# Linear attention and a gated feed-forward on one TensorE: the first two weight loads in parts of a tile of their own

## The chip, the cores and the metric

The kernel runs on one core of a Trainium2 chip. The metric is the device time in microseconds (us) of one execution; several executions are timed and the median is given. A profile is one execution more closely recorded, with a start and an end for the instructions of each engine: TensorE (PE, with its weight loads shown apart as PEld), VectorE (DVE), ScalarE (ACT), GpSimd (POOL) and SyncE (SP). A few matmul records can be missing from a trace.

## The reference

Two parts follow one another. First a linear attention over q, k and v of shape (8 batches, 8 heads, 576 positions, 64):

```python
q_s = softmax(q over the 64 channels)
k_s = softmax(k over the 576 positions)
kv  = einsum('bhsd,bhse->bhde', k_s, v)
x   = einsum('bhsd,bhde->bhse', q_s, kv)      # then (8, 576, 512)
```

Then a channel mix, with d_model 512 and d_ff 1024:

```python
x_prev = x shifted by one position
xk = mu_k * x + (1 - mu_k) * x_prev
xr = mu_r * x + (1 - mu_r) * x_prev
k  = relu(xk @ w_k)
out = sigmoid(xr @ w_r) * ((k * k) @ w_v)
```

## The kernel before

All inputs are float32 in the chip's memory; matmuls run in bf16 and accumulate in float32. The attention goes by batch b and by group g of four heads (g = 0, 1: 256 channels). For each, q, k and v are loaded into tiles raw_*, q and k go through exp on ACT (line 451), DVE sums and scales q (464 to 472), and TensorE transposes q (504) and forms kv (481). For the first two batches the mixing weights mu are folded into kv (561), so that TensorE itself delivers the mixed xk and xr (517), which ACT and DVE copy to the long tiles xk and xr (574). Later batches mix on DVE.

The feed-forward goes in units of up to 512 positions. A unit has k-matmuls (line 718) for eight blocks fc of 128 columns of w_k, each summed over four input tiles ct of 128 channels; ACT and DVE form the squared relu (703, 707); then come the r-matmuls (751), tanh (756), the v-matmuls (761), the gating (767) and the store (778). There are four PSUM banks mm_a to mm_d for these and two double ones, att_a and att_b, for the attention.

Which columns a block fc takes: those of one half of w_k's 1024 columns, in steps of four; blocks 0 to 3 take the first half, 4 to 7 the second. The channels ct 0 and 1 belong to group g = 0, ct 2 and 3 to g = 1. In the first two units ("early") the k-matmuls are planned for four blocks at a time: ct 0 and 1 of all four, then ct 2 and 3 of all four, so that they can start before group 1 is ready.

The order on each engine is not left to the program's order. Every operation is entered in a plan with an engine, an estimated time and its dependencies; `Plan.order` (133) simulates them and fixes one order for each engine. Beside this the compiler tracks which addresses of a tile an instruction reads and another writes, and puts in the semaphore waits.

Weights are loaded by POOL's DMA queue, which turns float32 into bf16 on the way, in the order of the list `LOADS` (35): raw_g's first half, wk0a, wk0b, wk1, raw_h's first half and so on. All POOL loads begin after the second half of raw_d has landed (`gate`, 387). wk0a and wk0b are the first and the second half of w_k's columns for g = 0 (ct 0 and 1); wk1 is all columns for g = 1. POOL's loads take eight completion semaphores in turn, so that a load waits for the landing of the one eight places before it. All of w_k lies in one tile, per partition ct by column:

```python
wk_bf = const.tile([128, CT, F], BF16, name="wk_bf")               # CT = 4, F = 1024
out=wk_bf[:, 2 * g:2 * g + 2, c:e]                                  # written by a load
lhsT=wk_bf[:, ct, F // 2 * (fc // 4) + fc % 4:F // 2 * (fc // 4 + 1):4]   # read by a k-matmul
```

In this layout wk0b writes columns 512 to 1023 of ct 0 and of ct 1: two pieces per partition. The first columns of ct 1 lie between the two pieces. In the compiled kernel TensorE's first wk weight load (ct 0, fc 0) waits for wk0a's semaphore, and the second (ct 1, fc 0), which reads only what wk0a has written, waits for wk0b's.

Of the kernel before, what the change touches and what calls it, by code (L numbers as in the profile page):

```python
# [13 lines left out]
BF16 = mybir.dt.bfloat16  # L14
# [20 lines left out]
LOADS = ("q10a", "wk0a", "wk0b", "wk1", "k10a", "q10b", "wr", "mu", "v10b", "v10a", "k10b",  # L35
         "wv0", "q11b", "wv1", "q11a", "k11b", "k11a", "v11a", "v11b")
# [172 lines left out]
def kernel(  # L209
# [12 lines left out]
    nc = tc.nc  # L222
# [3 lines left out]
    F = moe_w_k.shape[1]  # L226
    assert S == 576 and D == 64 and H == 8, f"{q.shape=}"
    J = S // 64
    CT = C // 128
# [13 lines left out]
    const = ctx.enter_context(tc.tile_pool(name="const", bufs=1))  # L243
# [28 lines left out]
    def bank(slot):  # L272
        return ps[slot.pool][slot.index][:]
# [4 lines left out]
        return bank(slot)[:, hf, :]  # L278

    xs = [const.tile([128, CT, RING], BF16, name=n) for n in ("xk", "xr")]  # L280
    wk_bf = const.tile([128, CT, F], BF16, name="wk_bf")
    wv_bf = const.tile([128, FT, C], BF16, name="wv_bf")
    wr_bf = const.tile([128, CT, C], BF16, name="wr_bf")
    mu_sb = const.tile([8, 128], F32, name="mu_sb")
# [105 lines left out]
    def emit_wk(g, c, e):  # L390
        ap = bass.AP(tensor=moe_w_k.tensor, offset=moe_w_k.offset + g * 128 * F + c,
                     ap=[[F, 128], [256 * F, 2], [1, e - c]])
        return nc.gpsimd.dma_start(out=wk_bf[:, 2 * g:2 * g + 2, c:e], in_=ap)

    def emit_wr():
        ap = bass.AP(tensor=moe_w_r.tensor, offset=moe_w_r.offset,
# [4 lines left out]
    for name in LOADS:  # L401
        if name.startswith("wk"):
            g = int(name[2])
            c, e = {"": (0, F), "a": (0, F // 2), "b": (F // 2, F)}[name[3:]]
            o = plan.add("POOL", 0.8, 0.8, LOADS.index(name),
                         lambda g=g, c=c, e=e: emit_wk(g, c, e), gate, size=1250.0 * (e - c) / F)
            for h in range(2):
                if c <= h * F // 2 < e:
                    wk_done[g, h] = o
# [281 lines left out]
    def unit(half, c0, n):  # L691
# [23 lines left out]

        def k_part(kf, fc, cts):
            for ct in cts:
                nc.tensor.matmul(bank(kf)[:, 0:n],  # L718
                                 lhsT=wk_bf[:, ct, F // 2 * (fc // 4) + fc % 4:F // 2 * (fc // 4 + 1):4],
                                 rhs=xs[0][:, ct, c0:c0 + n],  # L720
                                 start=(ct == 0), stop=(ct == CT - 1))

# [2 lines left out]
        for f0 in range(0, FT, step):  # L725
            kfs = [Slot("mm") for _ in range(step)]
            mms_ = [None] * step
            for cts in ((0, 1), (2, 3)) if early else (range(CT),):
                gs = sorted({ct // 2 for ct in cts})
                for i in range(step):  # L730
                    fc = f0 + i
                    mms_[i] = plan.add(
                        "PE", per * len(cts), per * len(cts) + 0.17, clock,
                        lambda kf=kfs[i], fc=fc, cts=cts: k_part(kf, fc, cts),
                        [o for b in bs for g in gs for o in mixed[b, g, 0]]
                        + [wk_done[h, fc // 4] for h in gs] + [mms_[i]],
                        [kfs[i]] if cts[0] == 0 else [])
                    clock += PACE * per * len(cts)
            for i in range(step):
                kdone.append(mms_[i])  # L740
                relu_square(f0 + i, kfs[i], mms_[i])
        rdone = []
        for m in range(n // 128):
            c = c0 + 128 * m
            rps, th, ot = Slot("mm"), Slot("th"), Slot("ot")
            parts = 2 if half == B // 4 - 1 and c + 128 == RING else 1
            w = C // parts
# [39 lines left out]
            for e in range(0, C, w):  # L787
                vps = Slot("mm")
                f = 1.0 / parts
# [66 lines left out]
```

## Time and profile before

| what | value |
|---|---|
| median of 5 runs | 202.4 us (201.28 to 202.75) |
| the five runs | 202.63, 201.28, 202.4, 202.75, 201.5 us |
| the profiled execution | 202.63 us, its span 200.7 us |
| wk loads: from issue to landing | 3.8, 6.0 and 8.3 us |
| weight loads of wk (line 718) | 320, median 113 ns |
| L718 matmuls, 512 columns | median 379 ns recorded |

The span runs from the first to the last recorded instruction; 1.9 us of the execution lie outside it. In the profile, a line of the timeline has the start, the duration, the engine, the line of the kernel, the operation, the output and inputs, how many instructions are merged in it, and in brackets the idle time of the engine before it and what ended that. A line of the chain has start, duration and what the time went to. A matmul's recorded duration is longer than the distance from one start to the next, since matmuls are pipelined: use distances between starts.

### The profile page before, as it was taken

Reading aid. Unit: us, or ns where it says so; the run is one execution under the profiler, and the core shown is the slowest. Engines: PE = TensorE matmul, PEld = TensorE weight load, DVE = VectorE, ACT = ScalarE, POOL = GpSimd, SP = SyncE. Lnnn points to the kernel's source line nnn. Section 1 sums busy time; section 2 is a strip of 40 time slices with the busy share of each in tenths; the row PEclk is TensorE's granted clock in tenths of the full one; section 3 lists DMA queues with packets and bytes.
Section 4 is the critical chain, followed back from the end, with each engine's and each line's share of the span. In section 5 each row is a group of like instructions: output and inputs, shape, how many; then the busy total and the mean of one; then the engine's idle time right before and its main releaser. Section 6 shows DMA issues by size and latency. Waiting matters only on the chain.

```text
span 200.7 us, 5314 instructions
## 1 busy us (share of the span) xinstructions
PE 184.1 (92%) x2147; PEld 96.7 (48%) x2171; DVE 160.6 (80%) x348; ACT 136.9 (68%) x212; POOL 40.5 (20%) x66
## 2 busy tenths in 40 slices
PE   2447999999999999999999999999999999999992
PEld 0234454545444555454466455455455544544761
DVE  2598469698999999999969999999998998432531
ACT  5593595898999789978559978946842662552440
POOL 1594375633154123411300000000000000000000
PEclk9999999999999999999999999999999999999999
DMA  6999999999999999993892220233042204402514
GB/s 190 359 273 222 301 259 369 392 398 414 385 401 405 407 390 332 391 371 111 256 352 65 52 58 0 52 88 74 3 96 65 52 3 105 105 0 52 118 42 105
DMA packets 15520, 40.72 MB, mean 203 GB/s; under 512 B 2300, under 2 KB 3592, under 8 KB 15496
## 3 DMA queue, kind: packets, MB, share of 16 engines
q0 software_dynamic: 7840, 27.40, 40.6%
q1 hardware_dynamic: 7208, 12.26, 21.3%
q10 hardware_dynamic: 448, 0.72, 1.3%
q8 instruction: 17, 0.28, 0.6%
q14 instruction: 7, 0.06, 0.1%
HBM read 33.56 MB, written 9.44 MB: 214 GB/s over the span
## 4 chain that ended last, share of the span: by engine, by line
PE 83%; DMA 11%; issue 1%; DVE 1%; POOL 1%; SPq 0%; ACT 0%; DVEq 0%
PE mm_c L761 9%; PE mm_a L718 9%; PE mm_d L718 9%; PE mm_d L761 7%; PE mm_a L761 7%; PE mm_c L718 7%; PE mm_b L761 6%; PE mm_b L718 6%; PE mm_b L751 5%; PE mm_d L751 4%; DMA out_dram<-ot_a 3%; PE mm_c L751 3%; DMA wk_bf<-in_moe_w_k_dram 3%; DMA raw_d<-in_q_dram 3%; PE mm_a L751 3%; PE att_b L517 2%
## 5 line engine op out<-in xcount | busy, mean ns | idle before, releaser
L718 PEld LDWEIGHTS <-wk_bf 128*128 128x128 bf16 x320 | 35.5, 114 | 27.9 <-issue 2.3
L718 PE MATMUL mm_a<-xk,wk_bf 128*128 128x512 bf16 (+1 forms) x96 | 24.3, 363 | 0.3 <-issue 0.2
L718 PE MATMUL mm_d<-xk,wk_bf 128*128 128x512 bf16 (+1 forms) x87 | 22.4, 370 | 0.3 <-DVE ot_a L767 0.2
L761 PEld LDWEIGHTS <-k_b 128*128 128x128 bf16 x152 | 14.5, 98 | 15.7 <-issue 0.7
L751 PEld LDWEIGHTS <-xr 128*128 128x128 bf16 x144 | 13.9, 98 | 15.9
L761 PEld LDWEIGHTS <-k_a 128*128 128x128 bf16 x144 | 13.4, 98 | 15.5 <-issue 0.4
L718 PE MATMUL mm_c<-xk,wk_bf 128*128 128x512 bf16 (+1 forms) x66 | 16.0, 358 | 0.4 <-DMA wk_bf<-in_moe_w_k_dram 0.3
L718 PE MATMUL mm_b<-xk,wk_bf 128*128 128x512 bf16 (+1 forms) x62 | 15.9, 360 | 0.2
L751 PE MATMUL mm_b<-wr_bf,xr 128*128 128x512 bf16 x50 | 13.3, 379 | 0.1
L761 PE MATMUL mm_c<-wv_bf,k_a 128*128 128x512 bf16 x46 | 12.1, 379 | 0.2 <-issue 0.2
L761 PE MATMUL mm_c<-wv_bf,k_b 128*128 128x512 bf16 x47 | 12.1, 379 | 0.2 <-issue 0.2
L756 ACT ACTIVATE th_a<-mm_b 128x512 f32<-128x512 f32 x12 | 7.1, 595 | 6.4 <-PE mm_b L751 4.9
L761 PE MATMUL mm_d<-wv_bf,k_b 128*128 128x512 bf16 x39 | 10.1, 379 | 0.2 <-issue 0.2
L761 PE MATMUL mm_b<-wv_bf,k_a 128*128 128x512 bf16 x38 | 10.0, 379 | 0.2 <-issue 0.2
L761 PE MATMUL mm_a<-wv_bf,k_b 128*128 128x512 bf16 (+1 forms) x39 | 9.4, 358 | 0.1
L751 PE MATMUL mm_d<-wr_bf,xr 128*128 128x512 bf16 x34 | 9.1, 379 | 0.1
L761 PE MATMUL mm_d<-wv_bf,k_a 128*128 128x512 bf16 x28 | 7.5, 379 | 0.4 <-issue 0.3
L707 DVE TENSOR_TENSOR k_a<-rel_b 128x512 bf16<-128x512 bf16 (+1 forms) x14 | 5.6, 397 | 2.8 <-ACT rel_b L703 2.8
L707 DVE TENSOR_TENSOR k_a<-rel_c 128x512 bf16<-128x512 bf16 (+1 forms) x13 | 5.1, 389 | 3.4 <-ACT rel_c L703 3.4
L756 ACT ACTIVATE th_b<-mm_c 128x512 f32<-128x512 f32 x6 | 3.7, 610 | 5.6 <-PE mm_c L751 4.7
L751 PE MATMUL mm_c<-wr_bf,xr 128*128 128x512 bf16 x28 | 7.2, 379 | 0.1
L751 PE MATMUL mm_a<-wr_bf,xr 128*128 128x512 bf16 x28 | 7.2, 379 | 0.0
(275 smaller groups left out, 416.7 us busy)
## 6 DMA issues: line engine op xcount, KB each, us to landing
out_dram<-ot_a SPq DMA_DIRECT2D x24, 128.0 KB, 3.7
out_dram<-ot_b SPq DMA_DIRECT2D x24, 128.0 KB, 3.1
out_dram<-ot_c SPq DMA_DIRECT2D x22, 128.0 KB, 3.0
raw_b<-in_k_dram POOLq DMA_DIRECT2D x3, 576.0 KB, 8.6
raw_c<-in_v_dram POOLq DMA_DIRECT2D x3, 576.0 KB, 8.2
raw_d<-in_q_dram POOLq DMA_DIRECT2D x3, 576.0 KB, 8.6
raw_a<-in_q_dram POOLq DMA_DIRECT2D x2, 576.0 KB, 10.6
raw_e<-in_k_dram POOLq DMA_DIRECT2D x2, 576.0 KB, 10.1
```

The costliest lines, as they stand in the source:

```text
L517: nc.tensor.matmul(bank(xp)[64 * hf:64 * hf + 64, u, at + c:at + e], lhsT=w[r, hf, :], rhs=qts[qt.index][r, hf, src:src + e - c], start=(n ...
L707: nc.vector.tensor_tensor(out=k2s[k2.index][:, fc, 0:n], in0=rels[rel.index][:, 0:n], in1=rels[rel.index][:, 0:n], op=ALU.mult)
L718: nc.tensor.matmul(bank(kf)[:, 0:n], lhsT=wk_bf[:, ct, F // 2 * (fc // 4) + fc % 4:F // 2 * (fc // 4 + 1):4], rhs=xs[0][:, ct, c0:c0 + n], ...
L751: nc.tensor.matmul(bank(rps), lhsT=xs[1][:, ct, c:c + 128], rhs=wr_bf[:, ct // 2 + 2 * (ct % 2), :], start=(ct == 0), stop=(ct == CT - 1))
L756: nc.scalar.activation(out=ths[th.index][:], in_=bank(rps), func=ACT.Tanh, scale=0.5)
L761: nc.tensor.matmul(bank(vps)[:, 0:w], lhsT=k2s[k2.index][:, ft, 128 * m:128 * m + 128], rhs=wv_bf[:, ft, e:e + w], start=(ft == 0), stop=( ...
```

## The change

The one tile for w_k becomes two, one for each group g. In the tile of g = 0, whose load is in two halves, each half of the columns has a part of its own, in one piece per partition: the half comes ahead of ct in the layout. The tile of g = 1 keeps columns together. The loads and the matmuls are the same in number, size and order; only addresses in SBUF differ, and the waits that the compiler puts in: one wait on TensorE, for wk0b, stands at the first weight load that reads wk0b's columns (ct 0, fc 4) instead of the second wk weight load.

```diff
-    wk_bf = const.tile([128, CT, F], BF16, name="wk_bf")
+    split = ["wk1a" in LOADS if g else "wk0a" in LOADS for g in range(2)]
+    wks = [const.tile([128, 2, 2, F // 2] if split[g] else [128, 2, F], BF16, name=f"wk_{g}")
+           for g in range(2)]
...
     def emit_wk(g, c, e):
         ap = bass.AP(tensor=moe_w_k.tensor, offset=moe_w_k.offset + g * 128 * F + c,
                      ap=[[F, 128], [256 * F, 2], [1, e - c]])
-        return nc.gpsimd.dma_start(out=wk_bf[:, 2 * g:2 * g + 2, c:e], in_=ap)
+        dst = wks[g][:, c * 2 // F, :, :] if split[g] else wks[g][:]
+        return nc.gpsimd.dma_start(out=dst, in_=ap)
...
         def k_part(kf, fc, cts):
             for ct in cts:
+                w, u, h = wks[ct // 2], ct % 2, fc // 4
                 nc.tensor.matmul(bank(kf)[:, 0:n],
-                                 lhsT=wk_bf[:, ct, F // 2 * (fc // 4) + fc % 4:F // 2 * (fc // 4 + 1):4],
+                                 lhsT=(w[:, h, u, fc % 4:F // 2:4] if split[ct // 2] else
+                                       w[:, u, F // 2 * h + fc % 4:F // 2 * (h + 1):4]),
                                  rhs=xs[0][:, ct, c0:c0 + n],
                                  start=(ct == 0), stop=(ct == CT - 1))
```

## The prediction

> **What bounds the kernel now.** I read the page's first and fourth parts, then the chain of waits in order of time, then PE's waits from 17 us on, and last the timeline of PE and its weight loads cut into slices so narrow that single instructions show.
>
> ```profile
> span 200.7 us, 5314 instructions
> PE 184.1 (92%) x2147; PEld 96.7 (48%) x2171; DVE 160.6 (80%) x348; ACT 136.9 (68%) x212; POOL 40.5 (20%) x66
> ...
> PE 83%; DMA 11%; issue 1%; DVE 1%; POOL 1%; SPq 0%; ACT 0%; DVEq 0%
> ```
>
> TensorE is the bound. The chain below starts with loads and becomes PE work at 18.1 us; PE's idle time after 17 us comes to 2 us in all. So whatever holds PE at 18 us is paid in full at the end.
>
> ```profile
> 10.38 0.74 POOL raw_g L308
> 11.12 0.70 POOL wk_bf L393
> 11.82 6.02 DMA wk_bf<-in_moe_w_k_dram
> 17.84 0.26 issue
> 18.10 0.63 PE mm_c L718
> 18.73 0.85 PE mm_d L718 x2
> ...
> PE mm_c L718 <- DMA wk_bf<-in_moe_w_k_dram: 0.3, 1, 0.3
> ```
>
> The load that ends at 17.84 is the second one issued, wk0b (issued at 11.82, after wk0a at 11.12); the tile's landing times are 3.8, 6.0 and 8.3 us, so wk0a was there at about 14.9. The first k-matmuls need only wk0a's columns. The wait row says that this false wait cost PE 0.34 us. Now the single instructions; "PEld" is a weight load:
>
> ```profile
> 17.69 0.11 PEld L718 LDWEIGHTS <-wk_bf 128*128 128x128 bf16 x1 [0.20 <-issue]
> ...
> 17.89 0.11 PEld L718 LDWEIGHTS <-wk_bf 128*128 128x128 bf16 x1
> ...
> 18.10 0.63 PE L718 MATMUL mm_c<-xk,wk_bf 128*128 128x512 bf16 x1 [0.34 <-DMA wk_bf<-in_moe_w_k_dram]
> ...
> 20.62 0.11 PEld L718 LDWEIGHTS <-wk_bf 128*128 128x128 bf16 x1 [0.20 <-issue]
> ...
> 20.63 0.13 PEld L718 LDWEIGHTS <-wk_bf 128*128 128x128 bf16 x1
> ...
> 21.03 0.63 PE L718 MATMUL mm_a<-xk,wk_bf 128*128 128x512 bf16 x1
> ```
>
> At 17.69 and 17.89 stand the weight loads of the first pair (input tiles ct 0 and 1 of mm_c). The matmul at 18.10 is the second of the pair: two weight loads came before it, and the first one's matmul has no record (311 of 320 L718 matmuls have one). At 20.62 the same pair of operations runs for mm_a, again just behind a run of L517 matmuls, and with nothing to wait for. There the second weight load starts 0.01 us after the first, not 0.20.
>
> **The change part by part.** The order of instructions is the same on all five engines of the two kernels, the same number of each kind. Exactly one thing differs: PE's second wk weight load no longer waits for wk0b; the first load that reads wk0b's columns (fc 4, ct 0) waits for it instead, 110 PE instructions later.
>
> *The wait that goes.* By the wait row it is worth 0.34 us, since PE continues as one chain from there: 202.3. By the start times it is worth nothing. Without a wait, the pair at 20.62 has its second matmul at 21.03 - 20.62 = 0.41 us after its first weight load. With the wait, the pair at 17.69 has it at 18.10 - 17.69 = 0.41 us after. The wait held the second weight load for 0.2 us, and the first matmul was running all that while: k-matmuls still start 0.43 us apart here (mm_a 20.62 to 21.03, then mm_b at 21.46). The wait row charges PE with a gap that is really the unrecorded matmul. A rule speaks for the second reading: the Trainium skill, "TensorE: Matmul & The Clock Gate", section "Step-by-step: what each phase is for", says that the next weights are loaded while the current matmul runs and that only weight loads move ahead of matmuls. By the wait row the sum is -0.34, by the rule and the two equal distances 0.00. I take 0.00, since it is measured on the same operations. The cover is thin, though. The second weight load takes 0.11 and began at 17.89; it could have begun at about 17.98 before the matmul at 18.10 came late (18.10 less the load's 0.11). That is 0.1 us of cover. In an execution where wk0b lands x later against PE's arrival, the wait costs x - 0.1.
>
> How large can x be? Both sides start from the same event: POOL begins its loads at 10.38 when raw_d has landed (10.1), and q and k of the same group, through exp, sum, transposition and the xk copies, bring PE to 17.69. So only wk0b's own 6.02 us on a crowded queue (the DMA share of 10 to 18 us is full) varies against it. Neighbours of like size (288 KB, same queue) took 5.9, 7.1 and 8.7 us; x is then from below 0 to some 1.1, by the 7.1 of raw_h, a load issued within 2 us of wk0b; the 8.7 belongs to loads queued behind all of wk and wr. A stall removed is worth 0 to 1.0; my value for the typical execution is 0.1.
>
> Behind the pair nothing is late that would eat a small gain. The L517 matmuls at 19.52 need att_a freed by ACT's copy, done at 17.80 + 0.64 = 18.44, 1.1 us early; mm_a and mm_b need two short DVE operations, done by 18.73; the weights wk1 are there at 12.5 + 8.3 = 20.8, needed at 23.06. A gain under 1 us passes to the end.
>
> *The wait that comes.* The load of fc 4 runs at 24.6 us; wk0b landed at 17.84, so the wait has been met for 6.8 us and is worth 0. That a weight load that carries a wait does not move ahead of a running matmul would cost at most one load, 0.11 us once, but the row at 17.89 shows just such a load running ahead of 18.10. Behind it on PE all is queued, but nothing is held.
>
> *The new layout.* wk0a and wk0b each write 2 KB in one piece per partition instead of two pieces of 1 KB. Cost from both sides: POOL's issue takes 0.74 us now, and fewer pieces could not make that longer. The nearest row is wk1, whose destination is in one piece already: in the trace its 256 packets are 2048 bytes each, one per row of the source, so pieces are not joined, and wk0a and wk0b should keep 256 packets of 1024 bytes. I take 0. A landing 0.5 us earlier would still give nothing, since PE does not wait for it any more. Later landing is the slow rival below. Weight loads read the same stride of four elements, 32 groups at a time, from another address: 0.11 us each as now, 320 times; 1 ns more on each would still be hidden, as PEld is busy 48%.
>
> Sum on the profiled execution: 200.7 of span plus 1.9 outside it = 202.63, less 0.0 for this execution. The median of the runs is 202.4; less the typical 0.1: **202.3 us**.
>
> **The rivals.**
>
> *The wait row is right* (a gain of 0.3 or a little more). For it: the row itself, and a chain that goes through this load. Against it: the two equal distances. If so, 202.4 - 0.34 = 202.06; with a landing 1 us later in the typical run, 202.4 - 1.0 = 201.4.
>
> *The tensor clock switches earlier.* The page's clock row shows full speed throughout, but the matmuls show the switch: 0.43 us apart up to mm_b at 21.89, and at 24.12 two in 0.43 us. The Trainium skill, the same page, section "What's actually happening", says that the clock doubles after about 3.4 us of sustained activity, counted in windows that run free of the kernel. No run here shows the windows. By the trace alone PE's start does not move, and so neither does the switch. By the rule, an execution whose window lacked only the stalled tenths could switch one window sooner: 3.4 us at half rate instead of full, 1.7 us won, 200.7 us. Against it: in this execution no activity moves except one weight load by 0.2 us. The same free phase would explain why the five runs lie at 201.3 to 201.5 and 202.4 to 202.75, a scatter that stays in both kernels.
>
> *Slower: the new layout makes wk0b land later.* POOL's second raw_i load waits for wk0b's landing (idle 1.40 us, issued at 18.12), because it takes over its completion semaphore. Behind it in POOL's queue are raw_h, wv and raw_j. ACT casts raw_i at 27.65 and about 28.2, and TensorE's L481 matmuls at 29.54 wait for what ACT does next. With 8.7 us the second raw_i lands at about 26.8 to 27.4, so some 1 us of slack; beyond that each us is a us. wk0b would have to take over 8 us instead of 6.02 for 202.4 + 1.0 = 203.4. wk1, twice as large, took 8.3. For it: PE no longer waits at wk0b, so nothing else would show it. Against it: the packets.
>
> **How the numbers follow.** No stall worth speaking of, 202.3, own range 201.6 to 202.9: 0.66. The wait or a later landing is worth 0.3 to 1.0, 201.4 to 202.1: 0.16, of which a third comes to 0.5% with the scatter. The clock switches sooner, about 200.7: 0.08. Slower through the landing or the layout, 203.4: 0.10. 0.5% is 1.0 us, about what a measurement of this kernel can tell from no change. Faster by more: the clock case 0.08, a third of the stall case 0.05 and scatter of the first case 0.03, 0.16. Slower by more: the slow case 0.10 and scatter 0.02, 0.12. Within: the rest, 0.72. The range reaches from the larger stall, 201.2, to near the slow case, 203.1.
>
> **What would show it right or wrong.** After the change the second wk weight load should stand within 0.02 us of the first, and the second matmul still 0.41 us behind the first load: right. If that distance falls under 0.35, the wait did cost. PE's row of waiting for the wk load should vanish, with the total idle as it was. wk0b should still land about 6 us after its issue, in 1024-byte packets, and raw_i be issued at about 18.1. I am wrong if the first k-matmuls come earlier relative to the L517 matmuls before them, if the half-rate stretch ends a window sooner in most runs, or if weight loads of the new tiles differ from 0.11 us.

## The result and the profile after

| | before | after |
|---|---|---|
| median | 202.64 us (80 runs) | 201.88 us (43 runs) |
| lowest and highest run | 201.13, 204.92 | 201.06, 203.17 |
| ratio of after to before | | 0.9967, 95% interval 0.9953 to 0.9981 |
| profiled execution, its span | 202.63, 200.7 | 201.88, 200.0 |

The changed kernel is faster by 0.33% (0.19% to 0.47%), some 0.7 us. That lies inside the forecast range of 201.2 to 203.1 us, and is several times the 0.1 us that the prediction gave the typical execution. Ratios leave out runs that lie more than 1.5% above the fastest of the same kernel, and so do the averages below, where this takes 18 of 202 runs from the kernel before and none of 67 from the changed one.

The page of the changed kernel, its head:

```profile
span 200.0 us, 5314 instructions
PE 184.0 (92%) x2147; PEld 96.7 (48%) x2171; DVE 160.8 (80%) x348; ACT 136.9 (68%) x212; POOL 40.7 (20%) x66
...
PE 85%; DMA 7%; DVE 3%; issue 1%; ACT 1%; SPq 0%; DVEq 0%
```

Busy times and counts are those of before, within 0.2 us. The DMA share of the chain went from 11% to 7%, mostly because the chain no longer goes through the wk load. The timeline of TensorE and its weight loads around 18 us, in narrow slices as before:

```profile
17.61 0.11 PEld L722 LDWEIGHTS <-wk 128*128 128x128 bf16 x1 [0.20 <-issue]
...
17.61 0.14 PEld L722 LDWEIGHTS <-wk 128*128 128x128 bf16 x2 [0.20 <-issue]
...
18.02 0.63 PE L722 MATMUL mm_c<-xk,wk 128*128 128x512 bf16 x1 [0.34 <-issue]
```

The second weight load now follows the first within 0.02 us (two loads in the 0.14 us from 17.61 on). The second matmul is at 18.02, 0.41 us behind the first weight load: exactly as before. The same 0.34 us of idle is recorded, only that its cause is now "issue": it was the matmul without a record. (In a later profile of the changed kernel, which has all 320 records, the first matmul stands at 17.50, the second 0.41 us behind, and no such idle time is listed.) So the profiled execution of before had really paid nothing for the wait.

Then why are the two spans 0.7 us apart? At 18 us the kernels are 0.08 us apart (18.10 and 18.02); from 24 to 104 us the distance between their weight loads stays at 0.04 to 0.06 us. The chain of each kernel around 100 us, first before:

```profile
96.61 6.75 DMA out_dram<-ot_a
...
105.66 0.40 PE att_a L517 x2
```

and after:

```profile
96.56 6.07 DMA out_dram<-ot_a
...
104.93 0.40 PE att_a L520 x2
```

A store of ot_a took 6.75 us in one and 6.07 us in the other. Its buffer was waited for, and TensorE's next L517 matmul came 0.73 us apart in place of 0.05. That is a transfer which the change doesn't touch. Subtracting the two profiles would give about the measured gain for a wrong reason.

### The profile page after: what moved, and what is told of

The parts are those of the page before. It is cut to its first block, busy times and chain, and to the rows that moved or that the text cites. A ratio compares the mean times of both kernels' runs of the same rounds, so it can differ in the third digit from the quotient of the medians.

```text
span 200.0 us, 5314 instructions
## 1 busy us (share of the span) xinstructions
PE 184.0 (92%) x2147; PEld 96.7 (48%) x2171; DVE 160.8 (80%) x348; ACT 136.9 (68%) x212; POOL 40.7 (20%) x66
## 3 DMA queue, kind: packets, MB, share of 16 engines
q1 hardware_dynamic: 7208, 12.26, 21.3%
## 4 chain that ended last, share of the span: by engine, by line
PE 85%; DMA 7%; DVE 3%; issue 1%; ACT 1%; SPq 0%; DVEq 0%
PE mm_c L766 10%; PE mm_a L722 9%; PE mm_d L722 9%; PE mm_d L766 7%; PE mm_a L766 7%; PE mm_c L722 7%; PE mm_b L766 6%; PE mm_b L722 6%; PE mm_b L756 5%; PE mm_d L756 4%; PE mm_c L756 3%; DMA out_dram<-ot_a 3%; PE att_b L520 3%; DMA raw_d<-in_q_dram 3%; PE mm_a L756 3%; PE att_a L520 3%
## 5 line engine op out<-in xcount | busy, mean ns | idle before, releaser
L722 PEld LDWEIGHTS <-wk 128*128 128x128 bf16 x320 | 35.5, 114 | 27.6 <-issue 2.2
L722 PE MATMUL mm_a<-xk,wk 128*128 128x512 bf16 (+1 forms) x96 | 24.3, 362 | 0.3 <-issue 0.2
L722 PE MATMUL mm_d<-xk,wk 128*128 128x512 bf16 (+1 forms) x87 | 22.4, 370 | 0.1
L722 PE MATMUL mm_c<-xk,wk 128*128 128x512 bf16 (+1 forms) x66 | 16.0, 358 | 0.4 <-issue 0.3
L722 PE MATMUL mm_b<-xk,wk 128*128 128x512 bf16 (+1 forms) x62 | 15.9, 360 | 0.2
```

Source lines behind the costliest of these rows:

```text
L722: nc.tensor.matmul(bank(kf)[:, 0:n], lhsT=(w[:, h, u, fc % 4:F // 2:4] if split[ct // 2] else w[:, u, F // 2 * h + fc % 4:F // 2 * (h + 1) ...
```

## The experiments

Theory A: the wait for wk0b costs time in executions where wk0b lands later than in the profiled one. Theory B: the new layout itself makes the gain. Theory C: it is a matter of which runs were compared. Theory A had two forms later: every tenth of the wait passes to the end (A1), or half of it while TensorE is still at half rate (A2).

### The wait put back, the layout kept

```diff
+                if early and c0 == 0 and fc == 0 and ct == 1:
+                    tc.add_manual_dep(mm.ins, wk_done[0, 1].made.ins.name, sync)
```

TensorE's second wk weight load waits for wk0b again; every wait and the order are those of before. Beside it ran the changed kernel and the kernel before, both unaltered.

> The changed kernel with one thing undone: the old wait is put back by hand, so that TensorE's second wk weight load waits for wk0b again, while the new layout stays. All other waits and the order of instructions are those of both kernels. Theory A (the wait costs in executions where wk0b lands late, though the profiled one showed no cost): as slow as before, ratio to before 1.000, and 0.3% above the changed kernel. Theory B (the new layout itself, its transfers or weight loads, makes the gain): as fast as the changed kernel, ratio 0.997. In its profile the second weight load stands behind the first by 0.015 us if wk0b is there, by more if not; the second matmul stands 0.41 us behind the first weight load where the wait is covered, by more where it costs.

> The changed kernel unaltered, for its time beside the others on one chip and for one more profile. Both theories: ratio to before 0.997 with an interval of about 0.002; if the gain of the first comparison was a matter of which runs were compared (theory C), 1.000. Profile: first weight load to second matmul 0.41 us.

> The kernel before unaltered, as a control of what this comparison can tell and for one more profile of it: ratio 1.000 by all theories. Theory A expects that profiles of it differ in the distance from the first wk weight load to the second matmul: 0.41 us when wk0b lands in time, up to 1.4 us when it lands late. Theory B expects 0.41 us in each.

Measured, 12 runs each: 202.55, 202.63 and 203.30 us, with ratios to before of 0.9999 (0.9962 to 1.0036), 0.9997 (0.9967 to 1.0026) and 1.0003 (0.9967 to 1.0039). The times tell nothing apart: twelve runs resolve 0.3%, which is the size of the effect. The profiles do. The timeline of weight loads in the repeat of the kernel before:

```profile
18.27 0.11 PEld L718 LDWEIGHTS <-wk_bf 128*128 128x128 bf16 x1 [0.20 <-issue]
19.23 0.15 PEld L718 LDWEIGHTS <-wk_bf 128*128 128x128 bf16 x2 [0.85 <-DMA wk_bf<-in_moe_w_k_dram]
```

and TensorE behind it:

```profile
19.24 0.62 PE L718 MATMUL mm_c<-xk,wk_bf 128*128 128x512 bf16 x1 [0.89 <-DMA wk_bf<-in_moe_w_k_dram]
```

In this execution wk0b landed 6.79 us after its issue (chain of waits below). The second weight load is 0.96 us behind the first, and the second matmul 0.97 us in place of 0.41: the wait cost 0.55 us. (The second matmul starts only 0.004 us after its weight load, so a load may start 0.41 us behind the first one before it costs anything.) The kernel with the wait put back, its weight loads:

```profile
17.87 0.11 PEld L722 LDWEIGHTS <-wk 128*128 128x128 bf16 x1 [0.20 <-issue]
18.70 0.15 PEld L722 LDWEIGHTS <-wk 128*128 128x128 bf16 x2 [0.72 <-DMA wk<-in_moe_w_k_dram]
```

and TensorE behind it:

```profile
18.71 0.61 PE L722 MATMUL mm_c<-xk,wk 128*128 128x512 bf16 x1 [0.77 <-DMA wk<-in_moe_w_k_dram]
```

Its second matmul came at 18.71, 0.84 us behind the first load: a cost of 0.43 us, in the new layout. In the changed kernel of the same comparison wk0b landed 8.3 us after issue, later than in any of these, and the pair stood 0.015 us apart, the second matmul 0.41 us behind. So the wait costs in some executions, and the change takes it away.

How much of the 0.55 us passes on is seen in the chain of the same repeat of before:

```profile
12.39 6.79 DMA wk_bf<-in_moe_w_k_dram
19.19 0.05 issue
19.24 0.62 PE mm_c L718
...
22.62 0.43 PE mm_b L718 x2
23.06 0.37 PE att_b L517 x8
23.43 0.25 PE att_a L517 x12
23.67 0.55 PE mm_c L718 x2
```

against the first profile of before:

```profile
21.67 0.85 PE mm_b L718 x2
22.52 0.37 PE att_b L517 x8
22.89 0.25 PE att_a L517 x12
23.13 0.55 PE mm_c L718 x2
```

The first wk weight load was 0.58 us later in the repeat (18.27, 17.69), the wait 0.55 us: 1.13 us in all. At the L517 matmuls the delay is 23.06 - 22.52 = 0.54 us, about half. The two mm_b matmuls tell why: 0.85 us in one, 0.43 in the other. TensorE went to full rate at the same time in both (22.38 and 22.33 in the trace's clock records), so the delayed work fell on the far side of the switch, where it takes half as long. That is form A2.

### The wait made longer

```diff
-  lambda g=g, c=c, e=e: emit_wk(g, c, e), gate, size=...)
+  lambda name=name: emit_wk(*{"wk0a": (0, 0, F // 2), "wk0b": (1, 0, F),
+                              "wk1": (0, F // 2, F)}[name]), gate, size=...)
```

POOL issues wk1 ahead of wk0b; the plan doesn't know of it, so all else stays in order.

> The kernel before with one edit: POOL issues wk1 (512 KB) ahead of wk0b, so that wk0b lands some 2 to 3 us later, at about 20.8; order and waits of all else are kept. The suspected wait made longer. Theory A: the second wk weight load stands about 2.5 to 3 us behind the first. If every tenth of that passes to the end (A1), 2.5 us over the changed kernel; if a delay before TensorE's switch to full rate costs half, because the switch comes at its own time and the work moved behind it runs at twice the rate (A2), about 1.3 us over the changed kernel, more only if the idle time puts the switch off as well. Theory B (layout): no slower than before, ratio 1.000.

> The changed kernel with the same edit, wk1 ahead of wk0b. wk0b is needed at 24.6 and wk1 at 23, so theory A (both forms) expects no cost: ratio to before 0.997 to 1.000, the pair of weight loads 0.015 us apart. If the late landing itself costs through POOL's queue (the slow rival of the prediction), as slow as the other kernel with this edit.

Measured: 206.27 us for the kernel before with this edit (ratio 1.0177, 1.0142 to 1.0212) and 202.39 us for the changed one (0.9987, 0.9959 to 1.0015). The chain of the former:

```profile
12.44 9.19 DMA wk_bf<-in_moe_w_k_dram
21.63 0.05 issue
21.67 0.61 PE mm_c L720
...
25.22 0.85 PE mm_b L720 x2
```

wk0b landed at 21.63, later than I had reckoned; the second matmul came 4.08 us behind the first weight load, a cost of 3.67 us. The difference between the two kernels' medians is 3.88 us. Here not half but all of the wait passes on, and the last row shows why: at 25.22 two matmuls still take 0.85 us. The switch came at 27.07 us in the clock records, after 22.4 before and 20.44 in the changed kernel with this edit. So A2's 1.3 us fails by its size; its reservation, that idle time may put the switch off, is what happened. The short wait above cost half, since the switch stayed where it was; this long one moved the switch too and cost its whole length. Theory B, by which the kernel before should have lost nothing, fails here.

The prediction's slow rival, a cost of a late wk0b through POOL's queue, is not excluded by it. In the changed kernel with this edit wk0b landed at 22.7 us in place of 17.3. Its 12 runs are 0.40 us above the mean of all runs of the changed kernel (95% interval 0.14 to 0.65), but 0.12 us (-0.20 to 0.43) above the 24 that were measured after the first comparison. In its profile POOL issues the second raw_i load, which waits for the load issued second (here wk1), at 21.7 us in place of 17.6. Between 25 and 49 us TensorE then loses 0.8 to 1.0 us against the changed kernel's first and third profile. Whether the one follows from the other was not tested.

### Matmuls without use ahead of the switch

If a gap puts the switch off, closing another gap should bring it forward. First come ten matmuls at 10 us, behind the first kv:

```diff
+            if b == 0 and g == 0:
+                for i in range(10):
+                    nc.tensor.matmul(ps["mm"][i % 2][:, 0:256], lhsT=ident[:],
+                                     rhs=ident[:, None, :].to_broadcast((128, 2, 128)),
+                                     start=True, stop=True)
```

> The kernel before with ten matmuls without use (256 columns each, on banks that are free then) put on TensorE behind the first kv at about 10 us, where it idles 2.3 us; order and waits of all else are kept. If TensorE's switch to full rate follows from its activity, it should come one or two steps of 3.4 us sooner than 22.4 (19.0 or 15.6), and save up to 1.7 us for each step of matmuls at half rate, if what feeds them keeps up: 200.5 to 202. With the switch ahead of the wk0b wait, theory A2 expects that the wait costs its whole length and is longer, since TensorE comes there sooner: 0.5 to 1 us over the next kernel. If the fillers only delay the transposes at 12.5: 202.6 or more.

> The changed kernel with the same ten matmuls. Theory A2: as the kernel before with them, less the whole wait, so 0.5 to 1 us faster than that one and the fastest of all, 199.5 to 201.5. Theory B or no effect of the change: the same as the kernel before with the ten matmuls.

Measured: 203.27 us (ratio 1.0015, 0.9983 to 1.0047) and 202.39 us (0.9994, 0.9963 to 1.0026). The times show no gain, and the switch is at 22.49 in the changed kernel with them. Its profile has a stop of 0.7 us at 77.6 us, too, which the next experiment explains. The 0.9 us between the two goes the way of theory A, but the intervals overlap. The profile of the first is from one of its longest executions (204.91 us) and is read by itself only: wk0b took 7.73 us to land, the wait cost 1.5 us, and the switch came at 25.28. It is a wait of that length with no edit to the loads.

Then come sixteen small matmuls (64 by 64, 256 columns, on mm_c and mm_d) in TensorE's gap ahead of 16.6 us, behind the attention matmuls (L517, in the changed kernel L520) for the first xk. In the profile of the changed kernel the gap is 0.73 us:

```profile
16.50 0.70 PE L520 MATMUL att_b<-qt_b,wp_c 64*64 64x288 bf16 x8 [0.73 <-ACT xk L577]
```

The edit:

```diff
+            if b == 0 and g == 0 and h == 0 and wp.index == 0:
+                for i in range(16):
+                    u, hf = i % 2, i // 2 % 2
+                    r = slice(64 * u, 64 * u + 64)
+                    nc.tensor.matmul(ps["mm"][2 + u][64 * hf:64 * hf + 64, 0:256], lhsT=ident[r, r],
+                                     rhs=ident[r, None, :].to_broadcast((64, 2, 128)), ...)
```

> The changed kernel with sixteen small matmuls without use (64 rows by 64, 256 columns, four side by side, on banks mm_c and mm_d, free by then) where TensorE idles some 0.9 us ahead of 16.6 us, between two runs of L517 matmuls; order and waits of all else are kept. If a stretch of 3.4 us without such a gap makes the switch to full rate, TensorE is now without one from 13.2 us, so that the switch comes between 17 and 21 us instead of between 20.4 and 22.5 in the profiles so far: about 2 us earlier, of which half is won, 1 us: 201 us. If not, 202 as the changed kernel.

> The kernel before with the same sixteen matmuls. The wait for wk0b still makes a gap at 18 us. Theory A: slower than the changed kernel with them, by at least 0.3 us if the switch comes at the same time, by 1.5 and more in executions where the wait's gap puts it off. Theory B: the same as the changed kernel with them.

Measured: 203.49 us (ratio 1.0040, 1.0008 to 1.0072) and 203.62 us (1.0031, 0.9996 to 1.0066). The switch did come forward, to 19.02 and 18.79 us, and yet neither kernel is faster than before; the first is slower, the second by an interval that just takes in 1. The timeline of the changed kernel with them has the reason, far from the edit:

```profile
75.10 0.82 PE L774 MATMUL mm_d<-wv_bf,k_a 128*128 128x512 bf16 x3
77.59 0.38 PE L774 MATMUL mm_d<-wv_bf,k_a 128*128 128x512 bf16 x1 [1.67 <-issue]
```

TensorE stops in the middle of four matmuls that wait for no other engine. The other kernel has the same stop, at the same instruction:

```profile
77.74 0.38 PE L769 MATMUL mm_d<-wv_bf,k_a 128*128 128x512 bf16 x1 [1.86 <-issue]
```

The changed kernel has none there. In the records of the queues of kind "instruction" a block of 16 KB begins to arrive between 74.1 and 77.7 us in every kernel, and takes 1.0 to 1.1 us. All fourteen profiles can be sorted by how long before TensorE's 991st weight load that is. In eleven, the kernels without added matmuls among them, the block begins 3.2 to 5.7 us ahead, and TensorE goes on without a stop. In the other three it begins 0.3 us (the kernel before with the sixteen), 0.4 us (the changed one with them) and 1.35 us ahead (the changed one with the ten). Just these three stop, each behind its 991st weight load, and each goes on 2.4 to 2.5 us after the block began to arrive. So I take the stop for TensorE waiting for its next instructions; the sorting leaves little room for another cause. Between the two kernels, A's 0.3 us and more was not found (0.13 us, within the noise), although the wait in the second cost 1.2 us in its profile; why it didn't show stays open.

The last run tests that reading with fewer instructions, three full-size matmuls in the place of the sixteen:

```diff
+            if b == 0 and g == 0 and h == 0 and wp.index == 0:
+                for i in range(3):
+                    nc.tensor.matmul(ps["mm"][2 + i % 2][:, 0:256], lhsT=ident[:],
+                                     rhs=ident[:, None, :].to_broadcast((128, 2, 128)),
+                                     start=True, stop=True)
```

> The changed kernel with three full-size matmuls without use (128 by 128, 256 columns) in the idle time ahead of 16.6 us, in place of the sixteen small ones: 6 more TensorE instructions, not 32. The sixteen brought the switch to 19.0 us but a stop of 1.7 us without a releaser at 75.9 us came with them. If that stop comes from the larger number of instructions ahead of it (TensorE waiting for its next block of instructions), it is gone or under 0.3 us here, and with a switch at 19 to 21 us the time is 201.2 to 201.8, 0.5 us under the changed kernel. If the stop is there again: 203. If three matmuls don't bring the switch forward: 202.1.

Measured: 201.18 us, ratio to before 0.9929 (0.9895 to 0.9963), the fastest of all. The timeline of TensorE:

```profile
15.87 0.39 PE L577 MATMUL mm_c<-ident 128*128 128x256 bf16 x1
16.06 0.38 PE L577 MATMUL mm_d<-ident 128*128 128x256 bf16 x1
16.27 0.27 PE L577 MATMUL mm_c<-ident 128*128 128x256 bf16 x1
16.66 0.44 PE L520 MATMUL att_b<-qt_b,wp_c 64*64 64x288 bf16 x8
16.91 0.44 PE L520 MATMUL att_a<-qt_b,wp_c 64*64 64x288 bf16 x12
17.28 0.62 PE L727 MATMUL mm_c<-xk,wk 128*128 128x512 bf16 x2
17.74 0.59 PE L727 MATMUL mm_d<-xk,wk 128*128 128x512 bf16 x2
```

Already the third of them is shorter (0.27), and the first k-matmuls take 0.46 us for two in place of 0.85: the switch is at 16.26 us. No stop is left around 75 us: four matmuls follow four without a gap, and the block of instructions begins to arrive 3.2 us ahead of the 991st weight load. In this kernel the wk1 weight loads begin at 20.92 us, where the changed kernel's began at 23.00. Of this lead of 2.1 us, 0.8 us is left at the end of the span (199.2 against 200.0).

### More executions of the wait

> The changed kernel with the old wait put back once more, for more executions: the first twelve had a median of 202.55 us, with four over 203.5. Theory A: the shape of before, a fifth or more of the runs over 203.5 us. Theory B: the shape of the changed kernel, none of its 55 runs so far over 203.5. In the profile the second weight load stands 0.2 to 1 us behind the first.

> The changed kernel unaltered, beside the last one on the same chip. Theory A: 0.2 to 0.7 us under it and no run over 203.5 us; theory B: the same as it. In the profile the pair of weight loads 0.015 us apart and the second matmul 0.41 us behind the first load, however late wk0b lands.

Measured: 202.44 us (ratio 0.9983, 0.9946 to 1.0020) and 202.35 us (0.9964, 0.9932 to 0.9995). The profile of the first is one where the wait was covered: second weight load 0.09 us behind the first, second matmul 0.41. All executions of the comparisons together, within the bound named above:

| kernel | runs | mean | median | over 203.5 us |
|---|---|---|---|---|
| before | 184 | 202.64 | 202.65 | 31 |
| new layout, wait put back | 22 | 202.59 | 202.32 | 5 |
| after | 67 | 202.06 | 202.07 | 0 |
| after, three matmuls in the gap | 12 | 201.37 | 201.18 | 0 |

After against the kernel with the wait put back: -0.52 us (95% interval -0.88 to -0.17, by resampling). That kernel against before: -0.06 us (-0.41 to 0.29). After against before: -0.58 us (-0.76 to -0.40). The three matmuls give -0.69 us more (-1.04 to -0.24), though the changed kernel did not run beside them.

Theory C has a part in the size of these differences: the changed kernel's first 43 runs average 201.91 us and its later 24 average 202.34. With the 24 alone, which ran beside the kernel with the wait put back, the difference of the means is -0.24 us (-0.65 to 0.16) and shows nothing. What holds there too is the last column: none of the 24 lies over 203.5 us, and 5 of the 22 do. Theory A holds, then. B is not needed, though a share of it of up to 0.4 us is not excluded.

What the long runs are can be worked out. In each of the fourteen profiles the clock records hold one stretch at full rate, and it lasts 177.49, 180.91 or 184.32 us: values 3.41 us apart, 52, 53 and 54 times 3.413. So both ends of the stretch lie on a grid with a step of 3.41 us. The far end can be estimated for each run whose mean granted clock is under 1, since the half rate at the end of the span is what lowers it; whole steps back from there give the switch, but for the number of steps. (In the eight profiles that allow it, the estimate is within 0.2 us of the clock record.) Sorted by this place, without the ends of the grid:

| switch at this place or a step of 3.41 us later | after | before, shorter runs | before, longer runs |
|---|---|---|---|
| 20 to 21 us | 13 runs, 201.1 to 202.1 | 13 runs, 201.2 to 202.0 | 11 runs, 203.3 to 204.1 |
| 21 to 22 us | 21 runs, 201.2 to 202.5 | 17 runs, 201.7 to 202.9 | 1 run, 204.1 |
| 22 to 23 us | 16 runs, 202.1 to 203.5 | 33 runs, 202.0 to 203.5 | none |

At the same place on the grid the kernel before has two kinds of runs and the changed kernel one. Measured from a straight line through the runs of the changed kernel (of the 54 with a known place, none lies more than 1.0 us above it), 15 of 85 runs of the kernel before lie 1.7 to 2.5 us above, none 1.0 to 1.7. So do 4 of 17 with the wait put back. A switch one step later leaves 3.41 us more at half rate, 1.7 us of time, and the wait itself comes on top: that is their size.

## Why the prediction was right, and where it was off

*The wait that goes.* The reading of the first profile held: two equal distances, so no cost in that execution; the changed kernel has the same 0.41 us. The wait row's 0.34 us was a missing record. The range held, but owing to its width of 1.9 us; the gain forecast was a sixth of the measured one. The step that failed is the size of the typical wait, "my value for the typical execution is 0.1". Over four executions with the wait (two of before, two with it put back) it cost 0, 0.55, 0.43 and 0 us, so 0.25 on average; the runs give a gain of 0.58 us. The bound of 0 to 1.0 was sound, and I placed the value near its lower end on the strength of one execution in which the cover happened to suffice. The cover was 0.2 us rather than 0.1, since a load that is waited for need be only 0.004 us ahead of its matmul; this made the wait look dearer, not cheaper. A cover that thin under a transfer of 6 us was the sign to take a middle value.

*A gain under 1 us passes to the end.* This step failed too, in both directions. TensorE was at half rate, and a delay ahead of its switch passes on by half if the switch stays (0.54 of 1.13 us) and by all of it if the switch moves (3.88 us for a wait of 3.67). I had both halves in hand, the switch at 22.4 and the rule on sustained activity in the Trainium skill, "TensorE: Matmul & The Clock Gate", section "What's actually happening", and used them for a rival only, instead of for the price of each tenth of the wait. The runs agree with that rule where it says that activity brings the switch: at 16.26 us in the profile with three matmuls in the gap. They show its free-running windows too: stretches at full rate in whole steps of 3.41 us, on a grid that lies differently in each execution. In the profiles of the two kernels, edits aside, the switch lies anywhere from 21.3 to 22.5 us.

*Where most of the gain comes from.* Half of 0.25 us is 0.12, not 0.58. The table of places accounts for the rest: 15 of 85 runs that are 2.1 us longer make 0.37 us in the mean, and the other 70 lie 0.2 us above the changed kernel's line, 0.18 us in the mean; together 0.55 us. That the 15 are executions in which the wait put the switch off by one step is inferred from the grid and their size. Switches that late were seen in the clock records when the wait was made longer (27.07 us) and in the kernel before with ten matmuls (25.28 us), but no profile of an unaltered kernel with the wait happened to be of such an execution.

*The wait that comes* cost nothing: in no profile of the changed kernel, with further edits or without, does TensorE wait for wk0b at fc 4. *The new layout* by itself cost and won nothing that the runs can tell: -0.06 us, with an interval of 0.35 to each side. *The slow rival*: wk0b landed 5.6, 8.3 and 6.2 us after its issue in three profiles of the changed kernel and 6.0 and 6.8 in two of before, which shows no later landing by the layout. That a late landing costs, as the rival had it, stays open: in the profile with 8.3 us, too, TensorE loses 0.8 us between 25 and 49 us. *The clock rival* was put too low: "an execution whose window lacked only the stalled tenths" is, by the inference above, what most of the gain is made of, in one run of six and not in the typical one.

## What to carry to other kernels

One profile shows whether a wait cost time in that execution, not what it costs on average: where the cover is thin against the transfer's own scatter, look at several profiles, or put the wait back in the new kernel and compare the spread of many runs, sorted by where the switch lay. Price a delay by the rate that TensorE has at that moment and by whether the delay moves its switch to full rate. And read idle time ahead of a matmul only after counting that all its neighbours have a record.

## What was not expected

Three matmuls without use, in a gap of some 0.7 us, brought the switch to full rate to 16.26 us in the profile, from 21.3 to 22.5, and 0.69 us of time; ten of them at 10 us, where other gaps follow, brought nothing that 12 runs can tell.

Thirty-two more TensorE instructions (sixteen weight loads and matmuls) brought a stop of 1.7 to 1.9 us some 60 us later, and turned a switch that came some 3 us sooner into a loss of 0.4% against before. Instructions arrive in blocks while the program runs (17 of 16 KB in each profile), and the stop falls behind the same weight load, the 991st, whatever was added. It came wherever its block had begun to arrive less than 1.4 us before that load, and nowhere with 3.2 us or more. The number of added instructions alone does not decide it: with the ten matmuls the changed kernel stopped for 0.7 us in its profile and the kernel before did not in its own. What sets the time of the block's arrival was not looked into.
